# Attention scores: each head on 64 rows of TensorE, three products of high and low parts, a pair's heads in the two halves of the array's rows

## The chip, the cores and the metric

The kernel runs on one core of a Trainium2 chip. Five engines work side by side, each through its own list of instructions in order: TensorE (PE, with its weight loads shown apart as PEld), VectorE (DVE), ScalarE (ACT), GpSimd (POOL) and SyncE (SP), which here issues the DMAs. They wait for one another by semaphores. The metric is the time of one execution on the device in microseconds: before the change the median of three runs is 624.03 us (623.66 to 625.28).

## What is computed

Attention over 2 batches, 8 heads, 576 positions and 64 features a head, with a bias made by a small network from the distance of two positions; then two layers of the form w_out(gate(w_in x)) on the 1152 rows that come out, with 512 features and 2048 hidden ones.

```python
scores = q @ k.T / sqrt(64)                    # per batch and head, 576 x 576
psi_rel = log1p(abs(i - j)); psi_i = log1p(max(i, 1))
bias = relu((psi_rel / psi_i)[..., None] @ w1 + b1) @ w2      # 32 hidden, one value a head
attn = softmax(scores + bias)                  # minus the row's maximum, + 1e-9 below
x = (attn @ v) as 1152 rows of 512
h = x @ moe_w_in;  x = (h * sigmoid(1.702 * h)) @ moe_w_out
h = x @ moe2_w_in; x = (P(h) / Q(|h|)) @ moe2_w_out           # P cubic, Q quadratic
```

All is float32. Products in the two layers and in the scores are made from parts: a value is split into a high part, rounded to the type float32r that PE takes at full rate, and the low rest, and high x high, high x low and low x high are added up.

## The kernel before

**Stages.** First the bias table is made: 36 "beats" (`beat`), each with hidden values on DVE, POOL and ACT, four products on PE in column quarters of the array, an evacuation, and a DMA into a table in DRAM, from which bias tiles `bt` come back. Between and after the beats run 40 attention steps (loop over `s` in `attention_moe_moe`). Then the two layers follow. The conversion of their weights (`conv`, `split`) runs beside them, and five conversions fall into attention steps.

**A step.** The steps take pairs of heads (`hp`, 0 to 3), batches (`b`) and blocks of 128 queries in the order 4, 0, 1, 2, 3 (`QORDER`). Block 4 holds the last 64 queries of both heads in one unit; the others have two units, one a head. From step 15 on five steps in a row have one pair and batch. In this text a cycle is such a row: A (block 4, steps 15, 20, 25, 30, 35), B (16, 21, 26, 31, 36), C, D and E.

In its list for step s PE has, in this order: the transpose of the tail columns of step s - 3 (L288), the scores of step s (L223), products with values of earlier steps (L350 at full width, L347 in two column halves of the array, as many as have come due), and the transposes of the probabilities of step s - 3 (L315). The order in time is thus L288, L223, L350/L347, L315, L288 of the next step. Values come due in groups of five at the end of blocks 1 and 3; a B step has none.

**Score tiles.** A unit's scores lie in a `wide` tile, two PSUM banks with 288 columns each. There are two such tiles in turn; the one for the first unit of a step also takes the tail transpose. DVE reads a tile in L243 (scores plus bias, and the row's minimum of the negated sum), then ACT takes the exponential (L247). A tile may be written again when DVE has read it. A DVE step runs, in order: L230 (of the step before, needs ACT's second exponential), L243 for head 0, the reciprocal L257, copies of the tail transposes (L297, or two small ones in L301 where step s - 3 was block 4), L243 for head 1, low parts of attention's output (L373), a conversion if one is due, the low part of a key (L201) if one is due.

**The operands before.** The input `qk` has each head's queries twice, one copy in partitions 0 to 63 and one in 64 to 127, and the keys twice in the same way. `q_high` rounds the whole of the queries to `qT`; `q_low` then puts the low part into the lower 64 partitions. So a column of `qT` is the high part above the low part of the same query, and one product of it with the high keys `khi` (both copies) gives high x high + low x high; one with the low keys `klo` gives high x low + low x low. A unit takes 2 halves x 2 products on all 128 rows. In block 4 both heads come into one tile by columns that are zero for the other head: 2 x 4 products. Parts are made one or two such rows of steps ahead: POOL the queries (L182, L187), ACT the high keys (L193), DVE the low keys (L201).

Of the kernel before, what the change touches and what calls it, by code (L numbers as in the profile page):

```python
# [40 lines left out]
BR = BW + 15  # L41


QW = 1216


class Attention:
# [114 lines left out]
    def load_qk(self, pb, part=None):  # L162
        if pb < 8:
            if part in (None, 0):
                self.raw[pb] = self.op.tile([128, QW + 2 * S], F32, tag="qk", name="qk", bufs=2)
            n = (QW + 2 * S) // 4
# [7 lines left out]

    def new_parts(self, pb):
        p, bufs = (self.pp, 1) if pb == 1 else (self.op, 2)
        self.qT[pb] = p.tile([128, QW], F32R, tag="qT", name="qT", bufs=bufs)
        self.khi[pb] = p.tile([128, 2, S], F32R, tag="khi", name="khi", bufs=bufs)
        self.klo[pb] = p.tile([128, 2, S], F32R, tag="klo", name="klo", bufs=bufs)

    def q_high(self, pb):
        self.nc.gpsimd.tensor_scalar(out=self.qT[pb][:], in0=self.raw[pb][:, 0:QW], scalar1=1.0, scalar2=1.0,  # L182
                                     op0=ALU.mult, op1=ALU.mult)
# [5 lines left out]
    def k_raw(self, pb, a):  # L189
        return self.raw[pb][:, QW + S * a:QW + S * a + S]  # L190

    def k_high(self, pb, a):
        self.nc.scalar.activation(out=self.khi[pb][:, a, :], in_=self.k_raw(pb, a), func=AF.Copy, scale=-0.125)  # L193

    def k_low(self, pb, a):
        k, hi, lo = self.k_raw(pb, a), self.khi[pb][:, a, :].bitcast(F32), self.klo[pb][:, a, :]
        if 2 * pb + a in ():
            self.nc.gpsimd.tensor_scalar(out=k, in0=k, scalar1=-0.125, scalar2=1.0, op0=ALU.mult, op1=ALU.mult)
            self.nc.gpsimd.tensor_tensor(out=lo, in0=k, in1=hi, op=ALU.subtract)
        else:  # L200
            self.nc.vector.scalar_tensor_tensor(out=lo, in0=k, scalar=-0.125, in1=hi, op0=ALU.mult, op1=ALU.subtract)  # L201


    def scores(self, s):
        nc = self.nc
        hp, b, qc = self.steps[s]
        pb = 2 * hp + b
        q, khi, klo = self.qT[pb], self.khi[pb], self.klo[pb]

        if qc < 4:  # L210
            units = [[(128 * qc, 0)], [(704 + 128 * qc, 1)]]
        else:
            units = [[(512, 0), (576, 1)]]
# [12 lines left out]
    def sums(self, s):  # L226
        if 0 <= s < len(self.steps):
# [301 lines left out]
def attention_moe_moe(tc, t):  # L529
    nc = tc.nc  # L530
    new = tc.alloc_tile_pool
    A, M = Attention(tc, t), Moe(tc, t)
# [23 lines left out]
    A.bt, A.raw, A.v, A.qT, A.khi, A.klo = {}, {}, {}, {}, {}, {}  # L556
# [20 lines left out]
    def beat():  # L577
        i = beats[0]
        beats[0] += 1
        if i >= 41:  # L580
            return
        if i == 2:
            A.bias_setup2()
        if 3 <= i < 39:
            A.bias_out(A.rows[i - 3])
        if 2 <= i < 38:
            A.bias_matmul(A.rows[i - 2])
        if i < 36:
# [6 lines left out]
        if i in (4, 6, 8, 11, 13, 15):  # L595
            pb, j = divmod((4, 6, 8, 11, 13, 15).index(i), 3)
            A.q_low(pb, QW * j // 3, QW * (j + 1) // 3)
# [24 lines left out]
    for s in range(n + TLAG + 2):  # L622
# [35 lines left out]
        for piece in (('ea', 'to', 'qh', 'eb', 'ql', 'kh', 'xa', 'su', 'cv', 'pv', 'tr', 'xb', 'no', 'vo', 'kl', 'vl') if s < 12 else ('ea', 'vo', 'su', 'pv', 'eb', 'qh', 'ql', 'kh', 'xa', 'tr', 'no', 'to', 'xb', 'vl', 'cv', 'kl')):  # L658
# [15 lines left out]
                        A.q_high(x)  # L674
            elif piece == 'kh':
                for x, part in prep:
                    if part in (1, 2):
                        A.k_high(x, (1, 2).index(part))
            elif piece == 'kl':
                for x, part in prep:  # L680
                    if part in (1, 2):
                        A.k_low(x, (1, 2).index(part))
            elif piece == 'ql':
                for x, part in prep:
                    if part in (1, 3):
                        j = (1, 3).index(part)
                        c = (0, 608, 1216)
                        A.q_low(x, c[j], c[j + 1])
            elif piece == 'xa':
                A.exps(s, 0)  # L690
            elif piece == 'xb':
# [141 lines left out]
def _layout(v):  # L833
    import numpy as np

    f = np.float32
    qk = np.zeros((8, 128, QW + 2 * S), f)
    vv = np.zeros((8, 128, 640), f)
    for hp in range(4):
        for b in range(2):  # L840
            q, k, x = (np.asarray(v[n])[b, 2 * hp:2 * hp + 2] for n in "qkv")
            o, q, k = qk[2 * hp + b], q.transpose(0, 2, 1), k.transpose(0, 2, 1)
            for h in (0, 64):
                o[h:h + 64, 0:576] = q[0]
                o[h:h + 64, 640:704] = q[1, :, 512:]
                o[h:h + 64, 704:QW] = q[1, :, :512]
                o[h:h + 64, QW:QW + S] = k[0]
                o[h:h + 64, QW + S:] = k[1]
# [46 lines left out]
```

## Time and profile before

| | |
|---|---|
| runs | 624.03 us median (623.66 to 625.28) |
| profiled execution | 624.78 us, span of its instructions 623.0 us |
| PE, PEld busy | 94%, 79% of the span |
| DVE, ACT, POOL busy | 70%, 71%, 63% |
| score products (L223) | 320, 92.4 us busy summed over their two groups |
| low keys on DVE (L201), high keys on ACT (L193) | 16 of 0.808 us, 16 of 0.694 us |
| queries on POOL (L182, L187 of 64x608) | 8 of 1.274 us, 12 of 1.490 us |
| load of a pair's queries and keys | 1184.0 KB |
| granted clock of PE | 0.99 on average |

Busy time is the union of an engine's instructions. Matmuls are pipelined, so one lasts longer than the distance to the next: that distance, start to start, is what a product costs PE. A name like `wide<-khi,qT` says tile written, tiles read. "[0.76 <-PE wide L223]" behind an instruction means that its engine stood idle for 0.76 us before it and that the score product released it.

### The profile page before, as it was taken

How to read it: one execution, taken by the hardware profiler on the slowest of the kernel's cores; microseconds unless marked ns; L12 is line 12 of the kernel's file. 1: busy time of each engine (PE TensorE's matmuls, PEld its weight loads, DVE VectorE, ACT ScalarE, POOL GpSimd, SP SyncE). 2: the span in 40 equal slices, each digit the busy share in tenths (PEclk: the TensorE clock that was granted, in tenths of full speed). 3: DMA queues.
4: the chain of work that ended last, by engine and by line, in shares of the span. 5: the costliest groups of instructions: out<-in, count | busy, mean ns of one | idle time of the engine just before them, and what ended most of it. 6: DMA issues, size and time to landing. Idle time of an engine off the chain costs nothing.

```text
span 623.0 us, 10326 instructions
## 1 busy us (share of the span) xinstructions
PE 588.4 (94%) x3450; PEld 494.7 (79%) x3450; DVE 437.4 (70%) x913; ACT 443.2 (71%) x921; POOL 394.4 (63%) x452
## 2 busy tenths in 40 slices
PE   6986999999999898899999989998999999999997
PEld 2233477777777887899999988987988899989995
DVE  7999876888876888821112888868778666666663
ACT  6777787899987666642222666678888987878784
POOL 5867668799974667732223577756767765655663
PEclk9999899999999999999999999998999999999999
DMA  6689781936414567610001476630100100001001
GB/s 241 176 279 290 212 328 31 391 128 240 141 34 136 176 211 217 205 38 0 2 1 34 129 209 204 204 102 1 35 1 1 51 2 1 0 1 52 1 1 51
DMA packets 23909, 70.93 MB, mean 114 GB/s; under 512 B 2480, under 2 KB 2864, under 8 KB 22960
## 3 DMA queue, kind: packets, MB, share of 16 engines
q1 hardware_dynamic: 23712, 70.15, 34.5%
q8 instruction: 27, 0.44, 0.3%
q14 instruction: 26, 0.21, 0.1%
q10 hardware_dynamic: 144, 0.13, 0.1%
HBM read 57.01 MB, written 13.25 MB: 113 GB/s over the span
## 4 chain that ended last, share of the span: by engine, by line
PE 37%; DVE 14%; ACT 13%; issue 2%; POOL 0%; DVEq 0%; ACTq 0%
PE hps L446 18%; PE acc L525 12%; PE acc L518 6%; DVE tmp L418 5%; ACT up L422 3%; ACT w L434 3%; DVE sg L465 2%; DVE tmp L425 2%; DVE top L423 2%; ACT sg L464 2%; ACT ra L489 1%; ACT sq L481 1%; ACT ra L488 1%; ACT ra L487 1%; ACT ra L484 1%
## 5 line engine op out<-in xcount | busy, mean ns | idle before, releaser
L446 PE MATMUL hps<-xhi,w 128*128 128x384 f32 x768 | 153.5, 341 | 14.5 <-DVE sg L465 9.9
L446 PEld LDWEIGHTS hps<-xhi,w 128*128 128x128 f32 x768 | 136.1, 189 | 24.8 <-DVE sg L465 15.6
L435 POOL TENSOR_TENSOR w<-tmp,w 128x512 fp32r<-128x512 f32 x64 | 82.5, 1288 | 40.2 <-ACT w L434 34.1
L458 POOL TENSOR_TENSOR glo<-sg,ghi 128x384 fp32r<-128x384 f32 x48 | 48.9, 1018 | 64.3 <-PE acc L518 45.0
L446 PE MATMUL hps<-xlo,w 128*128 128x384 f32 x384 | 82.2, 335 | 0.0
L518 PE MATMUL acc<-ghi,w 128*128 128x384 f32 x384 | 76.7, 334 | 0.0
L525 PE MATMUL acc<-w,ghi 128*128 128x512 f32 x288 | 75.7, 393 | 0.0
L465 DVE TENSOR_TENSOR sg<-hps,sg 128x384 f32<-128x384 f32 x48 | 26.8, 558 | 65.5 <-ACT sg L464 65.5
L260 POOL TENSOR_SCALAR p<-p,mn 128x512 f32<-128x512 f32 x72 | 57.4, 808 | 22.4 <-DVE PTt L297 9.2
L498 POOL TENSOR_SCALAR ra<-ra,small 128x384 f32<-128x384 f32 x48 | 28.2, 587 | 66.5 <-ACT ra L487 66.5
L247 ACT ACTIVATE p<-p,mn 128x576 f32<-128x576 f32 x72 | 55.9, 778 | 18.8 <-DVE mn L243 10.9
L446 PEld LDWEIGHTS hps<-xlo,w 128*128 128x128 f32 x384 | 68.3, 189 | 0.0
L518 PEld LDWEIGHTS acc<-ghi,w 128*128 128x128 f32 x384 | 67.5, 188 | 0.0
L422 ACT ACTIVATE up<-raw 128x512 int32<-128x512 uint32 x59 | 37.8, 641 | 36.5 <-DVE tmp L418 33.7
L243 DVE CUSTOM_DVE_ANT_0 p<-wide,bt 128x576 f32<-128x576 f32 x72 | 54.1, 751 | 8.8 <-PE wide L223 6.9
L525 PEld LDWEIGHTS acc<-w,ghi 128*128 128x128 f32 x288 | 53.4, 188 | 8.6
L497 DVE TENSOR_TENSOR ra<-ra,hps 128x384 f32<-128x384 f32 x48 | 26.6, 555 | 37.4 <-ACT ra L489 37.3
L455 ACT CAST ghi<-sg 128x384 fp32r<-128x384 f32 x48 | 24.7, 514 | 38.2 <-DVE sg L465 19.8
L500 POOL TENSOR_TENSOR ra<-ra 128x384 f32<-128x384 f32 x48 | 48.7, 1015 | 4.1
L458 POOL TENSOR_TENSOR glo<-ra,ghi 128x384 fp32r<-128x384 f32 x48 | 48.8, 1017 | 2.5 <-PE acc L525 2.0
L223 PE MATMUL wide<-khi,qT 128*128 128x288 f32 x160 | 48.1, 323 | 1.4 <-ACT st L137 0.8
L464 ACT ACTIVATE sg<-hps 128x384 f32<-128x384 f32 x48 | 23.4, 487 | 30.7 <-PE hps L446 30.7
(95 smaller groups left out, 1285.0 us busy)
## 6 DMA issues: line engine op xcount, KB each, us to landing
raw<-win SPq DMA_DIRECT2D x32, 512.0 KB, 3.6
raw<-wout SPq DMA_DIRECT2D x32, 512.0 KB, 3.7
bias_all<-st SPq DMA_DIRECT2D x36, 295.5 KB, 3.7
bt<-bias_all SPq DMA_DIRECT2D x16, 576.0 KB, 6.0
qk<-qk SPq DMA_DIRECT2D x7, 1184.0 KB, 7.5
v<-v SPq DMA_DIRECT2D x8, 320.0 KB, 5.7
out<-o SPq DMA_DIRECT2D x8, 256.0 KB, 2.2
qk<-qk SPq DMA_DIRECT2D x4, 296.0 KB, 4.2
```

The lines of the kernel that those rows point to most:

```text
L223: nc.tensor.matmul(ps[:, half, 0:288], w, x, start=(i == 0), stop=(i == len(ops) - 1))
L243: nc.vector.tensor_tensor_reduce(out=pv.rearrange("p (x j) -> p x j", x=2), in0=ps[:, :, 0:288], in1=self.bt[qc][:, a, :].rearrange("p (x ...
L247: nc.scalar.activation(out=pv, in_=pv, func=AF.Exp, bias=mn[:, a:a + 1], scale=-1.0, accum_out=mn[:, 2 + a:3 + a])
L260: nc.gpsimd.tensor_scalar(out=p[:, a, 0:512], in0=p[:, a, 0:512], scalar1=r, scalar2=1.0, op0=ALU.mult, op1=ALU.mult)
L422: nc.scalar.activation(out=self.up[j].bitcast(I32), in_=lo, func=AF.Copy, scale=2.0 ** -29)
L435: nc.gpsimd.tensor_tensor(out=w[:, 2 * o + 1, :], in0=val, in1=w[:, 2 * o, :].bitcast(F32), op=ALU.subtract)
L446: nc.tensor.matmul(ps[:, 0:CH], w[:, wi, 128 * d:128 * d + 128], xx[:, d, :], start=(i == 0 and d == 0), stop=(i == 2 and d == 3))
L458: nc.gpsimd.tensor_tensor(out=glo[:], in0=g, in1=ghi[:].bitcast(F32), op=ALU.subtract)
L465: nc.vector.tensor_tensor(out=sg[:], in0=h, in1=sg[:], op=ALU.mult)
L500: nc.gpsimd.tensor_tensor(out=t0[0][:], in0=t0[0][:], in1=t0[1][:], op=ALU.add)
L518: nc.tensor.matmul(acc[e][:, 0:CH], w[:, wi, 128 * e:128 * e + 128], g[gi][:], start=(k == 0 and i == 0), stop=(k == NF - 1 and i == 2))
L525: nc.tensor.matmul(acc[e][:], g[gi][:, 128 * e:128 * e + 128], w[:, wi, :], start=(k == 0 and i == 0), stop=(k == NF - 1 and i == 2))
```

## The change

The input has each head once: head 0 of a pair in partitions 0 to 63, head 1 in 64 to 127, queries (640 columns, the last 128 with zeros where the column is the other head's) and keys (576). Tiles `q` and `k` hold the high and the low part side by side. A head's scores are three products a half (high x high, low x high, high x low) on its 64 rows, at row position 0 or 64 of the array; the two heads' products are issued in turn, each into its own tile. Block 4 takes all 128 rows and one tile, as before, with three products a half. Low x low is left out. High and low parts are made in fewer and partly wider operations, and the conversions within the beats and steps move to fewer places.

```diff
-QW = 1216
+QW = 640
     def load_qk(self, pb, part=None):
...
-                self.raw[pb] = self.op.tile([128, QW + 2 * S], F32, tag="qk", name="qk", bufs=2)
+                self.raw[pb] = self.op.tile([128, QW + S], F32, tag="qk", name="qk", bufs=2)
     def new_parts(self, pb):
         p, bufs = (self.pp, 1) if pb == 1 else (self.op, 2)
-        self.qT[pb] = p.tile([128, QW], F32R, tag="qT", name="qT", bufs=bufs)
-        self.khi[pb] = p.tile([128, 2, S], F32R, tag="khi", name="khi", bufs=bufs)
-        self.klo[pb] = p.tile([128, 2, S], F32R, tag="klo", name="klo", bufs=bufs)
+        self.q[pb] = p.tile([128, 2, QW], F32R, tag="q", name="q", bufs=bufs)
+        self.k[pb] = p.tile([128, 2, S], F32R, tag="k", name="k", bufs=bufs)
     def q_low(self, pb, a, b):
-        q = self.qT[pb][64:128, a:b]
-        self.nc.gpsimd.tensor_tensor(out=q, in0=self.raw[pb][64:128, a:b], in1=q.bitcast(F32), op=ALU.subtract)
+        q = self.q[pb][:, :, a:b]
+        self.nc.gpsimd.tensor_tensor(out=q[:, 1, :], in0=self.raw[pb][:, a:b], in1=q[:, 0, :].bitcast(F32),
+                                     op=ALU.subtract)
+    def k_high(self, pb):
+        self.nc.scalar.activation(out=self.k[pb][:, 0, :], in_=self.raw[pb][:, QW:], func=AF.Copy, scale=-0.125)
+    def k_low(self, pb):
+        k = self.k[pb]
+        self.nc.vector.scalar_tensor_tensor(out=k[:, 1, :], in0=self.raw[pb][:, QW:], scalar=-0.125,
+                                            in1=k[:, 0, :].bitcast(F32), op0=ALU.mult, op1=ALU.subtract)
     def scores(self, s):
...
-        for unit in units:
+        heads = [slice(0, 64), slice(64, 128)] if qc < 4 else [slice(0, 128)]
+        for _ in heads:
             ps, self.stile = self.stile, None
-            if ps is None:
-                ps = self.wide()
-            for half in range(2):
-                sl = slice(288 * half, 288 * half + 288)
-                ops = [(q[:, o:o + 128], k[:, a, sl]) for o, a in unit for k in (khi, klo)]
-                for i, (w, x) in enumerate(ops):
-                    nc.tensor.matmul(ps[:, half, 0:288], w, x, start=(i == 0), stop=(i == len(ops) - 1))
-            self.sp.append(ps)
+            self.sp.append(self.wide() if ps is None else ps)
+        for half in range(2):
+            for i, (x, y) in enumerate(((0, 0), (1, 0), (0, 1))):
+                for ps, p in zip(self.sp, heads):
+                    nc.tensor.matmul(ps[:, half, 0:288], q[p, x, 128 * qc:128 * qc + 128],
+                                     k[p, y, 288 * half:288 * half + 288], start=(i == 0), stop=(i == 2),
+                                     tile_position=(p.start, 0))
 def attention_moe_moe(tc, t):
...
-        if i in (6, 8, 13, 15):
-            A.k_low(i // 10, int(i in (8, 15)))
-        if i in (5, 7, 12, 14):
-            A.k_high(i // 10, int(i in (7, 14)))
+        if i in (6, 13):
+            A.k_high(i // 10)
+        if i in (7, 14):
+            A.k_low(i // 10)
...
             elif piece == 'kl':
                 for x, part in prep:
-                    if part in (1, 2):
-                        A.k_low(x, (1, 2).index(part))
+                    if part == 2:
+                        A.k_low(x)
```

On PE, at step 32 (a C step), these are the instructions in order before the change; a number behind a tile's name tells one buffer's use from another's, and "waits" names the engines whose semaphores an instruction waits for.

```order
L288 MATMUL wide_2029<-cst_99,ptl_1915 128x128 [waits DVE_49,PE_49,Pool_49]
L223 MATMUL wide_2029<-khi_1718,qT_1717 128x288
L223 MATMUL wide_2029<-klo_1719,qT_1717 128x288
L223 MATMUL wide_2029<-khi_1718,qT_1717 128x288
L223 MATMUL wide_2029<-klo_1719,qT_1717 128x288
L223 MATMUL wide_2035<-khi_1718,qT_1717 128x288 [waits DVE_49]
L223 MATMUL wide_2035<-klo_1719,qT_1717 128x288
```

The same place on PE with the change (L279 is the tail transpose, L213 the score product):

```order
L279 MATMUL wide_2090<-cst_99,ptl_1976 128x128 [waits DVE_49,PE_49,Pool_49]
L213 MATMUL wide_2090<-k_1766,q_1765 128x288
L213 MATMUL wide_2092<-k_1766,q_1765 128x288 [waits DVE_49]
L213 MATMUL wide_2090<-k_1766,q_1765 128x288
L213 MATMUL wide_2092<-k_1766,q_1765 128x288
L213 MATMUL wide_2090<-k_1766,q_1765 128x288
```

Before, four products go to the first tile and the fifth, first into the second tile, waits for DVE. Now the tiles alternate, and the wait for the second tile stands at the second of twelve products.

On DVE in the bias stage, where it makes hidden values (L98) and low parts of the keys (L201 before, L194 now):

```order
 L98 TENSOR_SCALAR room<-bc,nbm 128x560 x3
 L98 TENSOR_SCALAR room<-bc,nbm 128x544 x3
-L201 SCALAR_TENSOR_TENSOR klo<-qk,khi 128x576
 L98 TENSOR_SCALAR room<-bc,nbm 128x528 x2
-L607 MEMSET small 128x1
+L194 SCALAR_TENSOR_TENSOR k<-qk,k 128x576
+L597 MEMSET small 128x1
 L98 TENSOR_SCALAR room<-up,nbm 128x512 x2
-L201 SCALAR_TENSOR_TENSOR klo<-qk,khi 128x576
 L98 TENSOR_SCALAR room<-up,nbm 128x496 x2
```

One operation of the same size stands where two did; the same happens for each later pair.

## Rows read from the trace of the kernel before

**Rows 1.** The page's first part: busy time, share of the span, instructions.
```profile
PE 588.4 (94%) x3450; PEld 494.7 (79%) x3450; DVE 437.4 (70%) x913; ACT 443.2 (71%) x921; POOL 394.4 (63%) x452
```

**Rows 2.** Stages: stretch, its length, busy us (instructions) by engine, PE's clock, DMA.
```profile
20.00:40.00 20.00, 18.40 (x117) 5.76 (x116) 20.00 (x38) 14.93 (x27) 15.14 (x21) 1.00 0.74 212
...
90.70:122.04 31.34, 31.34 (x229) 23.08 (x228) 23.00 (x76) 25.32 (x60) 23.75 (x31) 1.00 0.56 213
153.97:169.89 15.92, 15.92 (x119) 12.17 (x118) 13.27 (x44) 14.81 (x37) 15.46 (x19) 1.00 0.46 165
```

**Rows 3.** Waits with PE waiting, 85 to 184 us: us in total, times, longest.
```profile
PE wide L288 <- DVE mn L230: 0.5, 1, 0.5
```

**Rows 4.** Order of time on PE, steps 31 to 34: start us, us, instruction.
```profile
157.19 0.38 PE L223 MATMUL wide<-khi,qT 128*128 128x288 f32 x1
157.41 0.29 PE L223 MATMUL wide<-klo,qT 128*128 128x288 f32 x1
...
158.20 0.29 PE L223 MATMUL wide<-klo,qT 128*128 128x288 f32 x1
...
159.33 0.38 PE L223 MATMUL wide<-khi,qT 128*128 128x288 f32 x1
...
159.94 0.32 PE L223 MATMUL wide<-khi,qT 128*128 128x288 f32 x1
...
160.35 0.29 PE L223 MATMUL wide<-klo,qT 128*128 128x288 f32 x1
...
163.30 0.38 PE L223 MATMUL wide<-khi,qT 128*128 128x288 f32 x1
...
164.30 0.29 PE L223 MATMUL wide<-klo,qT 128*128 128x288 f32 x1
...
166.27 0.38 PE L223 MATMUL wide<-khi,qT 128*128 128x288 f32 x1
...
167.29 0.30 PE L223 MATMUL wide<-klo,qT 128*128 128x288 f32 x1
```

**Rows 5.** Order of time on DVE: reads of the score tiles, steps 31 and 33.
```profile
158.09 0.76 DVE L243 CUSTOM_DVE_ANT_0 p<-wide,bt 128x576 f32<-128x576 f32 x1 [0.76 <-PE wide L223]
...
159.04 0.75 DVE L243 CUSTOM_DVE_ANT_0 p<-wide,bt 128x576 f32<-128x576 f32 x1
...
164.20 0.76 DVE L243 CUSTOM_DVE_ANT_0 p<-wide,bt 128x576 f32<-128x576 f32 x1
...
164.96 0.44 DVE L301 COPY PTt<-wide 64x64 f32<-64x64 f32 x2
165.43 0.76 DVE L243 CUSTOM_DVE_ANT_0 p<-wide,bt 128x576 f32<-128x576 f32 x1
```

**Rows 6.** Order of time on PE around value products in column halves, step 23.
```profile
132.45 0.29 PE L223 MATMUL wide<-klo,qT 128*128 128x288 f32 x1
132.67 0.49 PE L347 MATMUL xt<-PT,v 128*64 128x320 f32 x2
...
133.53 0.44 PE L347 MATMUL xt<-PT,v 128*64 128x320 f32 x2
133.90 0.33 PE L315 MATMUL pt<-cst,p 128*128 128x128 f32 x1
```

**Rows 7.** Order of time around step 2: a release and two waits for it.
```profile
41.20 0.08 DVE L243 DVE_READ_ACCUMULATOR2_ANT mn<- 128x1 f32 x1
...
41.58 0.29 PE L223 MATMUL wide<-klo,qT 128*128 128x288 f32 x1
...
42.93 0.40 PE L223 MATMUL wide<-khi,qT 128*128 128x288 f32 x1 [0.79 <-ACT st L137]
...
42.98 0.76 DVE L243 CUSTOM_DVE_ANT_0 p<-wide,bt 128x576 f32<-128x576 f32 x1
```

**Rows 8.** Groups by line and shape: busy us, mean ns of one, idle before.
```profile
L223 PEld LDWEIGHTS wide<-khi,qT 128*128 128x128 f32 x160 | 31.1, 194 | 3.8 <-ACT room L91 1.2 <-DVE mn L243 1.2 <-ACT st L137 1.0
...
L201 DVE SCALAR_TENSOR_TENSOR klo<-qk,khi 128x576 fp32r<-128x576 f32 x16 | 12.9, 808 | 0.0
```

More of the change, by code (lines that the diff above doesn't have):

```diff
@@ L164, in load_qk @@
             if part in (None, 0):
-                self.raw[pb] = self.op.tile([128, QW + 2 * S], F32, tag="qk", name="qk", bufs=2)
-            n = (QW + 2 * S) // 4
+                self.raw[pb] = self.op.tile([128, QW + S], F32, tag="qk", name="qk", bufs=2)
+            n = (QW + S) // 4
             sl = slice(0, 4 * n) if part is None else slice(n * part, n * part + n)
@@ L176, in new_parts @@
         p, bufs = (self.pp, 1) if pb == 1 else (self.op, 2)
-        self.qT[pb] = p.tile([128, QW], F32R, tag="qT", name="qT", bufs=bufs)
-        self.khi[pb] = p.tile([128, 2, S], F32R, tag="khi", name="khi", bufs=bufs)
-        self.klo[pb] = p.tile([128, 2, S], F32R, tag="klo", name="klo", bufs=bufs)
+        self.q[pb] = p.tile([128, 2, QW], F32R, tag="q", name="q", bufs=bufs)
+        self.k[pb] = p.tile([128, 2, S], F32R, tag="k", name="k", bufs=bufs)
     def q_high(self, pb):
-        self.nc.gpsimd.tensor_scalar(out=self.qT[pb][:], in0=self.raw[pb][:, 0:QW], scalar1=1.0, scalar2=1.0,
+        self.nc.gpsimd.tensor_scalar(out=self.q[pb][:, 0, :], in0=self.raw[pb][:, 0:QW], scalar1=1.0, scalar2=1.0,
                                      op0=ALU.mult, op1=ALU.mult)
     def q_low(self, pb, a, b):
-        q = self.qT[pb][64:128, a:b]
-        self.nc.gpsimd.tensor_tensor(out=q, in0=self.raw[pb][64:128, a:b], in1=q.bitcast(F32), op=ALU.subtract)
[L189 to L201, printed above, removed]
+        q = self.q[pb][:, :, a:b]
[7 more added lines that the diff above has]
+                                            in1=k[:, 0, :].bitcast(F32), op0=ALU.mult, op1=ALU.subtract)
     def scores(self, s):
@@ L207, in scores @@
         pb = 2 * hp + b
[L208 to L213, printed above, removed]
+        q, k = self.q[pb], self.k[pb]
+        heads = [slice(0, 64), slice(64, 128)] if qc < 4 else [slice(0, 128)]
         self.sp = []
-        for unit in units:
+        for _ in heads:
             ps, self.stile = self.stile, None
-            if ps is None:
-                ps = self.wide()
-            for half in range(2):
-                sl = slice(288 * half, 288 * half + 288)
-                ops = [(q[:, o:o + 128], k[:, a, sl]) for o, a in unit for k in (khi, klo)]
-                for i, (w, x) in enumerate(ops):
-                    nc.tensor.matmul(ps[:, half, 0:288], w, x, start=(i == 0), stop=(i == len(ops) - 1))
-            self.sp.append(ps)
+            self.sp.append(self.wide() if ps is None else ps)
[5 more added lines that the diff above has]
+                                     tile_position=(p.start, 0))
     def sums(self, s):
@@ L555, in attention_moe_moe @@
     A.bd = dp.tile([S * H * BR + 16], F32, name="bias_all")
-    A.bt, A.raw, A.v, A.qT, A.khi, A.klo = {}, {}, {}, {}, {}, {}
+    A.bt, A.raw, A.v, A.q, A.k = {}, {}, {}, {}, {}
     A.P, A.mn, A.PT = {}, {}, {}
@@ L594, in beat @@
             A.q_high(i // 10)
-        if i in (4, 6, 8, 11, 13, 15):
-            pb, j = divmod((4, 6, 8, 11, 13, 15).index(i), 3)
-            A.q_low(pb, QW * j // 3, QW * (j + 1) // 3)
-        if i in (6, 8, 13, 15):
-            A.k_low(i // 10, int(i in (8, 15)))
-        if i in (5, 7, 12, 14):
-            A.k_high(i // 10, int(i in (7, 14)))
+        if i in (5, 8, 12, 15):
+            A.q_low(i // 10, 0 if i in (8, 15) else 320, 320 if i in (8, 15) else 640)
+        if i in (6, 13):
+            A.k_high(i // 10)
+        if i in (7, 14):
+            A.k_low(i // 10)
         if i in (21, 26, 34):
@@ L676, in attention_moe_moe @@
                 for x, part in prep:
-                    if part in (1, 2):
-                        A.k_high(x, (1, 2).index(part))
+                    if part == 1:
+                        A.k_high(x)
             elif piece == 'kl':
                 for x, part in prep:
-                    if part in (1, 2):
-                        A.k_low(x, (1, 2).index(part))
+                    if part == 2:
+                        A.k_low(x)
             elif piece == 'ql':
@@ L685, in attention_moe_moe @@
                     if part in (1, 3):
-                        j = (1, 3).index(part)
-                        c = (0, 608, 1216)
-                        A.q_low(x, c[j], c[j + 1])
+                        A.q_low(x, 320 if part == 1 else 0, 640 if part == 1 else 320)
             elif piece == 'xa':
@@ L836, in _layout @@
     f = np.float32
-    qk = np.zeros((8, 128, QW + 2 * S), f)
+    qk = np.zeros((8, 128, QW + S), f)
     vv = np.zeros((8, 128, 640), f)
@@ L842, in _layout @@
             o, q, k = qk[2 * hp + b], q.transpose(0, 2, 1), k.transpose(0, 2, 1)
[L843 to L848, printed above, removed]
+            for a in range(2):
+                h = slice(64 * a, 64 * a + 64)
+                o[h, 0:512] = q[a, :, :512]
+                o[h, 512 + 64 * a:576 + 64 * a] = q[a, :, 512:]
+                o[h, QW:] = k[a]
             vv[2 * hp + b, :, :512] = x[:, :512].reshape(2, 4, 128, D).transpose(2, 1, 0, 3).reshape(128, 512)
```

## The prediction, made before the changed kernel was run

> **What bounds the kernel now.** The page's busy line gives PE 94% of the span, the others 63 to 71% [rows 1], but a busy PE says little by itself, so I cut the span into the kernel's own stages. Three matter. In 20 to 40 us, where the bias table is made, DVE is busy for all of the 20 us and PE is not. From 90.70 us (step 11) to 169.89 us (step 35) PE is busy without a gap, ACT and POOL for over 90% of the later rows [rows 2]. The list of waits with PE as the waiting engine has, from 85 to 184 us, one entry of 0.5 us in all [rows 3]: there each step ends when PE is through its list, and what PE gains or loses is gained or lost by the kernel. After attention the two gated layers run in their own order and only begin sooner or later; the change touches nothing there.
>
> Then one cycle of five steps in PE's order of time [rows 4], 15.92 us long: A (one unit of two heads, query block 4), B, C, D, E (two heads each). In a step's eight score products the starts stand 0.132 us apart (157.41 to 158.20, six intervals). B is the short step: it starts at 157.19, has no value products, and C starts 2.14 later. Against it stand DVE's two reads of the score tiles [rows 5]: head 0's begins at 158.09, while head 1's products still run; head 1's begins 0.95 later and ends at 159.79. C's fifth product, the first that writes the tile head 1 lay in, starts at 159.94: only 0.15 later. So PE is the bound, but at the short step DVE is hardly behind it. That interleaving, head 0 finished halfway, is what the change gives up.
>
> **The change, part by part.** *Products.* A unit with one head had 2 x 2 products on 128 rows; now a head has 2 x 3 on 64 rows, and the two heads are issued in turn. If two such run together, a step takes six slots instead of eight: 2 x 0.132 = 0.264 us saved per step, also in A, where six products on all rows replace eight. For steps 11 to 39 that is 29 x 0.264 = 7.7 us. Do two halves run together? The trace has no row halves, but column halves: two value products start together at 132.67 and two more at 133.53, and the last two take 0.44 together, hardly more than one [rows 6]. I take row halves to behave likewise.
>
> *Changes of array shape.* Before, scores, transposes and the tail transpose shared one shape, and only the value products had another. Where shapes change, the next product starts 0.22 after the last score product (132.45 to 132.67) instead of 0.13, and the first pair lasts 0.49 where a later one lasts 0.44. Back again it is 133.53 to 133.90, 0.37, against 0.29 between pairs ((133.53 - 132.67)/3) [rows 6]. So a change costs about 0.09 + 0.05; call it w = 0.15, with 0.05 (only the longer first product) and 0.25 (the 0.16 by which a product's 0.29 outlasts its slot, and 0.09) as ends. The new scores add a change at the entry of each two-headed step, and one at the exit where transposes or the full-width value product follow, since an exit to column halves was a change already. Per cycle that is 4 + 3.
>
> *The wait that moves.* Before, the first four products write one tile and the fifth waits for the other tile to be read. Now the second of twelve waits for it. Queued behind it on PE are ten products, then values and transposes; ACT's copies of the transposes and DVE's next first read wait for those. Also DVE's first read now waits for the whole step. I walk one cycle, times from B's start, first for B. First pair effectively at 0.09 + w (before, 0.09: 157.41 less 0.132), last pair 0.66 later at 0.90, end 1.19 (0.29 each), first read 1.31 (0.12 after the end, as 158.09 stands to the fourth product, which started at 157.68 and took 0.29). The second read ends 1.70 after the first begins [rows 5]: 3.01. Now C: a product behind such a wait is effectively under way 0.17 after the release (41.28, end of the read's accumulator, to 41.58 less 0.132 [rows 7]). So 3.18, and C's last pair starts at 3.84, where C's last product started at 160.35 - 157.19 = 3.16: 0.68 late. The exit adds w: D starts 0.83 late. D needs no wait, and its last pair is at 0.90 for 1.00, so E is 0.72 late by PE; but D's second read ends 1.99 after its first begins (164.20 to 166.19, two small copies lie between), at 1.31 + 1.99 = 3.30 from D's start, and E's last pair then starts at 3.30 + 0.17 + 0.66 = 4.13 where it started at 167.29 - 163.30 = 3.99. E is 0.97 late, its exit makes 1.12, A gives back 0.26: **0.86 us lost per cycle**. In general 0.26 + 4w; even changes of shape for nothing would not make it a gain.
>
> Four cycles (20 to 39) lose 3.4. Steps 11 to 19 (31.34 us, [rows 2]) have longer steps between and one short step, 13. The same walk gives -0.78 + 8w = +0.4. Together 0.26 + 24w: 3.9 us, and 1.5 to 6.3 for the ends of w.
>
> *The bias stage.* DVE makes the low part of the keys in 8 instead of 16 operations of 0.81 us [rows 8]. Three of those that go lie before step 11, at most 2.4 us of a full DVE. Against it: at step 2 head 1's tile comes free only for the product at 42.93, and head 0's read follows at 42.98 [rows 7]; it would now begin 0.11 + 0.66 + 0.29 + 0.12 after 42.93, at 44.11, 1.1 later. In the steps that follow each other directly (7, 8) the second read and the next first read are now at least 0.17 + 0.66 + 0.29 + 0.12 = 1.24 apart; I put 0.4 on each, an estimate. I take -2.4 + 1.1 + 0.8 = -0.5, with -2.4 and +2 as ends.
>
> *Taken at nothing:* the halved load of queries and keys on SP's queue, ACT's high parts of the keys (8 fewer), POOL's high and low parts of the queries (fewer elements; the low part in a shape the trace lacks, 128x320 for 64x608). All end before PE asks for them [rows 3]; without that cover they would be gains.
>
> Sum: 3.9 - 0.5 = +3.4 on the profiled execution's 624.78 us (span 623.0 and 1.8 around it), 628.2. The median of the runs is 0.75 lower, so **627.4**.
>
> **Rivals.** *(1) PE alone decides: faster.* If reads end before PE asks, a short step costs no wait, and only products less changes count: 7.7 - 39w (23 entries and 16 exits). With w between the row's 0.15 and its low end, 0.10, that is -3.8, with the bias part -4.3: 619.7. For it: one PE wait in 99 us, and outside the short step and the one after it the second tile is free well before it is asked for. Against it: the 0.15 us margin at C. It decides as soon as DVE's second read ends about 0.7 us sooner than in my walk, for instance because PE's lead moves to another step.
>
> *(2) The halves don't run together,* so the change doesn't do what it says. Twelve slots of 0.132: a step's last product at 1.69, B's second read ends at 3.67, C is 2.0 late; the same walk gives 3.5 per cycle, 14 for four, 5 for steps 11 to 19, and 1 in the bias stage: +20, 644. For it: no row shows row halves. Against it: the column halves.
>
> *(3) A head's next weights load only after its product.* Today products on the same rows follow at 0.132 although each has a load of 0.19 [rows 4, 8], so loads hide beneath products of the same rows. If that fails for halves, a pair takes 0.132 and some 0.11 (of the 0.17 behind a release): six of 0.24, last pair at 1.44, 3.0 per cycle, 12 for four, 4.5 and 1: +17, 641. For it: halves load in turn, twelve loads where there were eight. Against it: those rows. The Trainium skill ("TensorE: Matmul & The Clock Gate", Part 3, What overlaps and what doesn't) says that a weight load overlaps running products only where their row groups differ; that would be this rival. By that rule the trace should not show 0.132 today, so I give it little.
>
> **How the numbers follow.** Forecast 0.62 at 627.4, its own range 624.5 to 630; rival 1 0.25 at 619.7; rival 2 0.07; rival 3 0.06. The range of 617.5 to 632 leaves out rivals 2 and 3 and the outermost of rival 1, some 0.16 to 0.19. The bound of what can be told is 0.3%, 1.9 us: below 622.2 or above 625.9. Most of rival 1 is faster, and a little of the forecast (a dear gain in the bias stage): 0.27. Of the forecast about a quarter lies within, with w near 0.05 to 0.10, and the slow end of rival 1: 0.18. The rest, 0.55, is slower.
>
> **What would show it.** Right: two score products with starts a few ns apart, one on each tile; PE waits named after DVE's second read, about 0.8 us at the step after B and 0.3 at E; cycles near 16.8 us instead of 15.92; first reads 0.4 us later in their step. Rival 1: cycles below 15.9 and no such wait. Rival 2: starts of all twelve 0.13 apart. Rival 3: pairs 0.24 apart with loads between. Wrong altogether: the stage before step 11 or the two layers after attention change by more than 2 us, or PE's granted clock falls in steps 11 to 39, where it is 1.00 now [rows 2].

## The result

The changed kernel takes 629.4 us, median of four runs (629.05 to 630.97), against 624.54 of the kernel before (four runs): a ratio of 1.0083, 95% interval 1.0060 to 1.0106, so 5 us slower. The forecast was 627.4, and 629.4 lies near the slow end of its own range. The profiled execution took 630.97 (span 629.2), 6.2 more than the one of before. Where these 6.2 us arise is read from the start of each step's score products, after less before, in the two traces:

| step | 2 | 3 | 10 | 20 | 25 | 30 | 35 | 39 | span |
|---|---|---|---|---|---|---|---|---|---|
| after - before, us | -3.30 | -1.74 | -1.27 | -0.21 | +1.60 | +3.50 | +5.39 | +6.12 | +6.2 |

Up to step 10 (the bias stage) 1.3 us are gained, steps 10 to 39 lose 7.4, and the two layers change nothing.

The page's first part, the three stages of [rows 2] (20 to 40 us, steps 11 to 19, one cycle from step 30 to 35), and the waits of PE:

```profile
PE 591.3 (94%) x3562; PEld 488.2 (78%) x3562; DVE 430.6 (68%) x905; ACT 439.6 (70%) x913; POOL 375.0 (60%) x450
```
```profile
20.00:40.00 20.00, 16.31 (x105) 5.24 (x105) 19.53 (x40) 16.05 (x32) 12.81 (x23) 1.00 0.82 246
89.73:121.86 32.13, 31.93 (x254) 21.36 (x253) 20.87 (x74) 24.13 (x57) 19.39 (x31) 1.00 0.48 171
157.50:175.31 17.81, 16.98 (x132) 11.37 (x133) 13.65 (x43) 14.35 (x36) 12.57 (x19) 1.00 0.39 144
```
```profile
PE wide L279 <- DVE PTt L288: 2.9, 6, 0.7
PE pt L306 <- ACT PT L322: 0.4, 2, 0.2
```

POOL has 19 us less to do than before [rows 1], and its share of a cycle falls from 15.46 of 15.92 us [rows 2] to 12.57 of 17.81. PE, which before was busy through the whole cycle, now idles 0.83 us of it at full clock, and its listed waits behind DVE are 2.9 us in place of 0.5 [rows 3], all at the tail transpose; a wait inside a step's row of score products does not stand in this list. A cycle is 17.8 us; forecast was 16.8.

PE's order of time over that cycle, for [rows 4]:

```profile
160.41 0.27 PE L279 MATMUL wide<-cst,ptl 128*128 128x128 f32 x1
160.61 1.05 PE L213 MATMUL wide<-k,q 64*128 64x288 f32 x12
...
163.19 1.41 PE L213 MATMUL wide<-k,q 64*128 64x288 f32 x12
...
167.63 1.06 PE L213 MATMUL wide<-k,q 64*128 64x288 f32 x12
...
170.54 1.38 PE L213 MATMUL wide<-k,q 64*128 64x288 f32 x12
...
173.49 1.09 PE L306 MATMUL pt<-cst,p 128*128 128x128 f32 x8
175.25 0.30 PE L279 MATMUL wide<-cst,ptl 128*128 128x128 f32 x1 [0.67 <-DVE PTt L288]
```

Twelve products take 1.05 us, six pairs: 5 x 0.13, 0.1 for the longer first one, and 0.29 for the last. The halves run together. Where PE must wait for the second tile (C at 163.19, E at 170.54) they take 1.41 and 1.38: 0.35 of waiting each. And A, the step after E, does not start its tail transpose until 175.25, 0.67 after the transposes of E are done. DVE's two reads before C's products, for [rows 5]:

```profile
161.79 0.76 DVE L234 CUSTOM_DVE_ANT_0 p<-wide,bt 128x576 f32<-128x576 f32 x1 [0.47 <-PE wide L213]
...
162.74 0.74 DVE L234 CUSTOM_DVE_ANT_0 p<-wide,bt 128x576 f32<-128x576 f32 x1
```

The first starts only when the whole step's products are through (161.67), the second ends at 163.49 with its accumulator, and C's second product starts at 163.55, 0.36 after its first: the wait that the prediction put there. For the wait behind E the rows of DVE and POOL, first before (step 34 starts at 166.27), then after (it starts at 170.54):

```profile
168.08 0.15 DVE L230 TENSOR_SCALAR mn<-mn 128x2 f32<-128x2 f32 x1
```
```profile
164.57 1.48 POOL L187 TENSOR_TENSOR qT<-qk,qT 64x608 fp32r<-64x608 f32 x1
166.15 2.56 POOL L260 TENSOR_SCALAR p<-p,mn 128x512 f32<-128x512 f32 x2
...
169.04 1.28 POOL L435 TENSOR_TENSOR w<-tmp,w 128x512 fp32r<-128x512 f32 x1
```
```profile
172.93 1.24 DVE L221 TENSOR_SCALAR mn<-mn 128x2 f32<-128x2 f32 x1
174.09 0.74 DVE L234 CUSTOM_DVE_ANT_0 p<-wide,bt 128x576 f32<-128x576 f32 x1
```
```profile
167.94 0.87 POOL L186 TENSOR_TENSOR q<-qk,q 128x320 fp32r<-128x320 f32 x1
169.85 1.36 POOL L251 TENSOR_SCALAR p<-p,mn 128x512 f32<-128x512 f32 x2 [1.04 <-DVE mn L248]
...
172.85 1.31 POOL L426 TENSOR_TENSOR w<-tmp,w 128x512 fp32r<-128x512 f32 x1 [0.84 <-ACT w L425]
```

Before, POOL was behind: low part, normalising, and only then (169.04) the subtraction that splits a converted weight; DVE's addition of 1e-9 to two columns of numbers had been done at 168.08 in 0.15 us. After, POOL's low part is 0.6 us shorter, it stands ready when the normalising can begin and again when the weight's high part is there, and starts the subtraction at 172.85, 0.08 us ahead of DVE's addition. That now lasts 1.24 us, and it ends 0.02 us after the subtraction (174.15 and 174.18). Step E's first read of a score tile starts 1.1 us late, and the chain of reads, tail copy and tail transpose carries it to PE. A weight is converted in steps 23, 28 and 33, and the addition lasts 1.24 us each time; the steps E behind them (24, 29, 34) are 4.77, 4.80 and 4.77 us long where they were 3.63, 3.63 and 3.65.

The trace of before has the same hold in another place, behind POOL's low part of the queries, in step 4 (and, 1.15 us long, in step 11), so its price could be read there:

```profile
59.58 1.47 POOL L187 TENSOR_TENSOR qT<-qk,qT 64x608 fp32r<-64x608 f32 x1
```
```profile
59.61 1.47 DVE L230 TENSOR_SCALAR mn<-mn 128x2 f32<-128x2 f32 x1
```

### The profile page after: what moved, and what is told of

Same layout as the page of the kernel before. It is cut to its first block, busy times and chain, and to the rows that moved or that the text cites. A ratio compares the mean times of both kernels' runs of the same rounds, so it can differ in the third digit from the quotient of the medians.

```text
span 629.2 us, 10515 instructions
## 1 busy us (share of the span) xinstructions
PE 591.3 (94%) x3562; PEld 488.2 (78%) x3562; DVE 430.6 (68%) x905; ACT 439.6 (70%) x913; POOL 375.0 (60%) x450
## 4 chain that ended last, share of the span: by engine, by line
PE 36%; DVE 14%; ACT 13%; issue 2%; POOL 0%; DVEq 0%; ACTq 0%
PE hps L437 18%; PE acc L516 12%; PE acc L509 6%; DVE tmp L409 5%; ACT up L413 3%; ACT w L425 3%; DVE sg L456 2%; DVE tmp L416 2%; DVE top L414 2%; ACT sg L455 2%; ACT ra L480 1%; ACT sq L472 1%; ACT ra L479 1%; ACT ra L478 1%; ACT ra L475 1%
## 5 line engine op out<-in xcount | busy, mean ns | idle before, releaser
L251 POOL TENSOR_SCALAR p<-p,mn 128x512 f32<-128x512 f32 x72 | 51.8, 730 | 46.1 <-DVE PTt L288 23.0
L213 PE MATMUL wide<-k,q 64*128 64x288 f32 (+1 forms) x432 | 48.9, 319 | 2.1 <-ACT st L137 1.2
L213 PEld LDWEIGHTS wide<-k,q 64*128 64x128 f32 (+1 forms) x432 | 36.9, 191 | 11.4 <-DVE mn L234 3.4
```

The lines of the kernel that those rows point to most:

```text
L213: nc.tensor.matmul(ps[:, half, 0:288], q[p, x, 128 * qc:128 * qc + 128], k[p, y, 288 * half:288 * half + 288], start=(i == 0), stop=(i == ...
L251: nc.gpsimd.tensor_scalar(out=p[:, a, 0:512], in0=p[:, a, 0:512], scalar1=r, scalar2=1.0, op0=ALU.mult, op1=ALU.mult)
```

## The experiments

The theory has two parts. **Collision:** about a third of the loss is POOL's subtraction holding DVE's small addition. **Waits:** the rest is PE waiting for the second tile at the short step and after it, and changes of array shape. The table gives each kernel's median, its ratio to the kernel before (which ran beside each, 624.15 to 624.62), what steps 10 to 39 cost in its profile against before, and the lengths of steps 24, 29 and 34.

| kernel | median us | ratio, 95% interval | steps 10 to 39 | E steps |
|---|---|---|---|---|
| changed | 629.40 | 1.0083 (1.0060 to 1.0106) | +7.4 | 4.77, 4.80, 4.77 |
| conversions in C | 627.67 | 1.0056 (1.0042 to 1.0070) | +5.1 | 4.07, 3.92, 3.91 |
| values even | 633.23 | 1.0149 (1.0133 to 1.0165) | +8.1 | 4.77, 4.78, 4.77 |
| heads in turn | 631.72 | 1.0128 (1.0107 to 1.0150) | +9.4 | 4.40, 4.41, 4.38 |
| both of the first two | 636.33 | 1.0192 (1.0179 to 1.0205) | +11.6 | 5.17, 3.91, 5.17 |
| low part three times | 627.86 | 1.0051 (1.0032 to 1.0070) | +5.1 | 4.08, 4.08, 3.90 |
| no small addition | 627.25 | 1.0038 (1.0023 to 1.0053) | +4.6 | 3.90, 3.90, 3.90 |
| that, values even | 627.75 | 1.0045 (1.0029 to 1.0060) | +3.3 | 3.77, 3.77, 3.76 |
| before, low part left out | 627.11 | 1.0037 (1.0020 to 1.0053) | +2.4 | 4.41, 4.43, 4.42 |
| no addition, tails first | 626.70 | 1.0043 (1.0029 to 1.0058) | +3.9 | 3.81, 3.82, 3.82 |
| that, values even | 625.54 | 1.0017 (1.0008 to 1.0027) | +2.9 | 3.73, 3.75, 3.74 |
| before, the same three | 626.15 | 1.0038 (1.0021 to 1.0056) | +2.0 | 3.68, 3.68, 3.68 |

The intervals of "conversions in C" and "low part three times" overlap with that of the changed kernel, so these two are told from it by the last two columns and not by the medians alone.

### Conversions one step earlier

```
-  for _ in range(n - s in (3, 7, 12, 17, 21) ...     # weight conversions
+  for _ in range(n - s in (3, 8, 13, 18, 21) ...
-  if part == 2:                        # low part of the keys
+  if part == (3 if s >= 20 else 2):
```

> Changed kernel, with the three weight conversions of steps 23, 28 and 33 (D) made one step earlier (C), and the low key parts made one step later to make room on DVE. Theory (collision: DVE's 1.24 us on 128x2 numbers lies inside POOL's two-input subtraction of the weight split, so step E's first read and with it PE comes about 1.1 us late, in three cycles): about 3 us faster than the changed kernel, 626, and no PE wait of 0.6 us behind the tail copy at step E. Rival (the conversion's own DVE work is what makes the step late, wherever it stands): it only moves to the step after, 0 to 1 us faster, 628.4 to 629.4.

Measured: 627.67, 1.7 us less, and in the profile 2.2 us less over steps 10 to 39. The addition at E is short again:

```profile
169.10 0.15 DVE L221 TENSOR_SCALAR mn<-mn 128x2 f32<-128x2 f32 x1
```

E is 3.9 to 4.1 us long and two of the three cycles are 16.95 and 16.97, close to the 16.8 of the prediction. The gain is smaller than the 3 us expected, since E without a collision is 0.87 shorter and not 1.1: PE's own work takes over first.

### Value products spread evenly, and with the first edit

```
-  for _ in range(5 if s >= n or len(pv) > 5 else ... 3 if pv and pv[0][1] == 4 else 2):
+  for _ in range(5 if s >= n or len(pv) > (6 if s >= 15 else 5) else 3 if s < 15 and pv and pv[0][1] == 4 else 2):
```

> Changed kernel, with the value products from step 15 on spread two chunks a step over all five steps, so that the short step B is no longer without them; the same instructions in all. Theory (the second of twelve products waits at C and E for the second tile since B is too short for DVE's two reads): the wait at C goes, 0.5 to 0.9 us a cycle, over four cycles 2 to 4 us faster than the changed kernel, 625.5 to 627.5. Rival (the loss is the changes of array shape, which this does not touch, or even one more of them in B): no change or up to 1 us slower, 629 to 630.5.

> Both edits together: conversions one step earlier and value products spread two a step. Theory (two separate losses, collision and short step): the gains add, 5 to 7 us faster than the changed kernel, 622.5 to 624.5, at or just below the kernel before. Rival (both edits ease one and the same wait): no more than the larger of the two alone, 625.5 to 627.

Both were wrong: 633.23 and 636.33, slower than the changed kernel. The wait at C did go (its products take 1.06 again), but B with value products is 3.14 us in place of 2.60 and C only 0.88 shorter, so the two steps gain 0.3. In both kernels 2.6 to 2.8 us are lost behind step 39, where more value products are left over and the first layer starts later. And the collision came at more places: also in step 38 of both, and in the second in each D behind a conversion:

```profile
168.40 1.24 DVE L221 TENSOR_SCALAR mn<-mn 128x2 f32<-128x2 f32 x1
```
```profile
168.02 1.59 POOL L426 TENSOR_TENSOR w<-tmp,w 128x512 fp32r<-128x512 f32 x1 [0.55 <-ACT w L425]
```

Here POOL began 0.4 us ahead (its subtraction itself took 1.59 in place of 1.28), and those steps D are 4.5 us long in place of 2.91, with a wait of 1.4 us on PE. In steps 24 and 34 the granted clock stands at its lower level (0.50, 1.2 GHz) for 3.4 us soon after that wait, and E is 5.17 us long; in step 29, at 1.00, it is 3.91. So in this kernel some 2.5 us of the 11.6 are clock, an estimate (2 x 1.26). Moving the conversion only shifts when the two meet; a few tenths decide.

### Heads one after the other

```
-  for half in range(2):
-      for i, (x, y) in enumerate(((0, 0), (1, 0), (0, 1))):
-          for ps, p in zip(self.sp, heads):
+  for ps, p in zip(self.sp, heads):
+      for half in range(2):
+          for i, (x, y) in enumerate(((0, 0), (1, 0), (0, 1))):
```

> Changed kernel, with head 0's six products issued first and then head 1's six, so that no two halves stand side by side; the same products. Theory (a pair of halves side by side takes one slot of 0.132 us): twelve slots in place of six, 0.53 us more than the eight of before in each of 23 two-headed steps from step 10 on, 0.26 less in six others, and the changes of shape 39 x 0.15: 16.5 us over before from step 10 on, where the changed kernel has 7.4; 638. Rival (side by side brings little, since the step is set by DVE's two reads): 629 to 631, or less, since head 1's tile is asked for later.

Measured: 631.72, between the two. The theory's 638 was wrong about the array:

```profile
163.30 1.43 PE L213 MATMUL wide<-k,q 64*128 64x288 f32 x12
```

Twelve in a row would take 11 x 0.132 + 0.29 = 1.74; here it is 1.43, against 1.05 in pairs. By the spacing of the single records and the two signals at the ends of the heads, head 0's six start at 163.30, .54, .67, .79, .93 and 164.07, and head 1's at 163.67, .91, 164.05, .18, .31 and .44: head 1's first product, issued seventh, started ahead of head 0's fourth. The records do not name the head; which is which is read from two regular rows of starts 0.13 apart and from the weight load that waits for the second tile, at 163.67. So 0.37 us a step are lost where PE is the bound (D is 3.28 for 2.91) and nothing where it waits anyway: C is 4.46 for 4.43, because the later second tile costs its 0.35 of waiting no more, and E is 4.40 for 4.77. From step 20 to 35 this kernel takes 53.51 us, the changed one 53.45; it is slower in steps 10 to 19 (1.5 us) and before.

### The collision, approached from four sides

More work for POOL in D, without the small addition, and before with less work for POOL:

```
   elif piece == 'ql': ...  if part in (1, 3):
+      for _ in range(3 if part == 3 else 1):
           A.q_low(...)
```
```
-  A.sums(s - 1)
-  nc.vector.reciprocal(out=mn[:, 6:6 + nu], in_=mn[:, 4:4 + nu])
+  nc.vector.reciprocal(out=mn[:, 6:6 + nu], in_=mn[:, 2:2 + nu])
```
```
   # kernel before
-  if part in (1, 3):
+  if part == 1 or (part == 3 and s < 20):
       ... A.q_low(...)
```

> Changed kernel, with POOL's low part of the queries in step D written three times over in place of once: 1.7 us more work for POOL in each cycle, the same results. Theory (POOL, relieved, comes to the weight split just as DVE comes to its small addition, and holds it 1.24 us): with POOL later, the addition goes first, step E is 3.9 us long in place of 4.8 in three cycles, and more work makes the kernel 2.2 to 2.7 us faster than the changed one, 626.7 to 627.2. Rival (POOL's load as such delays what follows): 629.4 or slower, up to 632.

> Changed kernel without DVE's small addition (1e-9 to sums that are at least 1, which changes no sum in fp32); the reciprocal reads the sums themselves. Theory (POOL's two-input operation holds only the small operation on two operands in SBUF, not the read of the score tile out of PSUM): step E 3.9 us in place of 4.8, 2.5 to 3 us faster than the changed kernel, 626.4 to 626.9. Rival (POOL holds whatever DVE brings next): the first read at E starts as late as now, no change, 629 to 629.4.

> Kernel before, scores untouched, with POOL's low part of the queries in step D left out from step 20 on (the low parts of half the query columns are then missing from the output). Theory (the collision needs nothing of the new scores, only POOL early at the weight split): the small addition is held 1.2 us in steps 23, 28 and 33, E is longer by up to 1.1 us in three cycles, and with less work the kernel is 2 to 3 us slower, 626 to 627. Rival (the collision needs the later reads of the new scores as well): no change, 623.8 to 624.5.

Measured: 627.86, 627.25 and 627.11. Giving POOL 1.7 us more to do in a cycle makes the kernel 1.5 us faster by the medians and 2.3 over steps 10 to 39; taking 1.5 us from POOL in the kernel before, with its old scores, makes it 2.5 us slower. All three lie on the theory's side, 0.1 to 0.7 us above its ranges. The three profiles, first DVE and POOL with the low part three times, then DVE and POOL without the addition, then DVE and POOL of before with the low part left out:

```profile
169.92 0.15 DVE L221 TENSOR_SCALAR mn<-mn 128x2 f32<-128x2 f32 x1
```
```profile
165.26 2.76 POOL L186 TENSOR_TENSOR q<-qk,q 128x320 fp32r<-128x320 f32 x3
168.00 2.55 POOL L251 TENSOR_SCALAR p<-p,mn 128x512 f32<-128x512 f32 x2
...
170.89 1.28 POOL L426 TENSOR_TENSOR w<-tmp,w 128x512 fp32r<-128x512 f32 x1
```
```profile
169.82 0.69 DVE L416 SCALAR_TENSOR_TENSOR tmp<-raw,tmp 128x512 uint32<-128x512 uint32 x1
170.43 0.75 DVE L234 CUSTOM_DVE_ANT_0 p<-wide,bt 128x576 f32<-128x576 f32 x1
```
```profile
170.37 1.28 POOL L426 TENSOR_TENSOR w<-tmp,w 128x512 fp32r<-128x512 f32 x1 [0.87 <-ACT w L425]
```
```profile
169.12 1.24 DVE L230 TENSOR_SCALAR mn<-mn 128x2 f32<-128x2 f32 x1
170.28 0.74 DVE L243 CUSTOM_DVE_ANT_0 p<-wide,bt 128x576 f32<-128x576 f32 x1
```
```profile
169.06 1.28 POOL L435 TENSOR_TENSOR w<-tmp,w 128x512 fp32r<-128x512 f32 x1 [0.86 <-ACT w L434]
```

With POOL late, the order is that of before: addition at 169.92, subtraction at 170.89. Without the addition, the read of the score tile out of PSUM starts at 170.43, while POOL's subtraction runs (170.37 to 171.65), and takes its usual 0.75: POOL holds the small operation, not the read. And the old scores show the same 1.24 us as soon as POOL is early, at 0.06 us ahead. That is cause and effect from both sides. The size in the changed kernel is 2.3 to 2.8 us of the 7.4.

The Trainium skill ("SBUF — State Buffer", SBUF: two separate sides) states that VectorE and GpSimd share one pair of ports as an exclusive lock: of a GpSimd operation and a VectorE operation that is in a two-port mode or has two inputs in SBUF, whichever starts first keeps the pair for its whole length, and the other is blocked in full. This case agrees for the addition: 1.24 us for an operation of 0.15, ending 0.02 to 0.03 us after POOL's. In which mode the addition runs no trace here shows.

### What is left: waits or changes of shape

```
-  'xa', 'tr', 'no', 'to', 'xb'     # first read .. tail copy, second read
+  'to', 'xa', 'tr', 'no', 'xb'
```

The even spread of value products was tried on top of the kernel without the addition and on top of this one, and all three edits on the kernel before. In the last two of these the spread ends with step 34, so that nothing more is left over behind step 39.

> As the kernel without the small addition, and with the value products spread two chunks a step. Theory (in the run with even value products the gain at C was there, 0.3 us over B and C, and was lost to the collision, which then also stood in step 38): cycles of 16.2 to 16.5 us in place of 16.95, four of them, 624 to 625.5, level with the kernel before. Rival (the extra change of shape in B eats what the wait gives): cycles of 16.9, 626.5 to 627.

> Changed kernel without the small addition, and from step 12 on DVE copies the transposed tails (0.27 us, in step D two copies, 0.44) before the first read of a step instead of between the two reads; the same work. Theory (what is left of the loss is PE's waits for the tiles that DVE reads: in a cycle about 0.37 us at the tail transpose before C, 0.35 at C's second product, 0.33 at E's): tiles come free 0.2 to 0.45 us sooner, 0.4 to 0.7 us a cycle, cycles of 16.2 to 16.5 in place of 16.9, 624.5 to 625.7. Rival (the rest is changes of array shape): cycles stay at 16.9, 627 to 627.5.

> The same, and value products two a step from step 15 to 34. Theory (waits and collision gone, PE's own work decides; PE's cycle is 5 x 0.26 shorter by the pairs and 7 or 8 changes of shape of 0.17 longer): cycles of 15.9 to 16.2, 622.5 to 624.5, level with or just below the kernel before. Rival (an eighth change of shape in B and what is left of the waits): cycles of 16.4 or more, 625 to 626.

> Kernel before with the same three edits (no small addition, tails copied first, values two a step from 15 to 34), scores untouched. Theory (it waits for no tile in steps 11 to 39, so there is nothing to gain): within 1 us of the kernel before, 623.5 to 625.2, a change of shape more in B against a little in the bias stage. Rival (the edits are good in themselves): 1.5 us or more faster.

Measured: 627.75, 626.70, 625.54 and 626.15. In the first, cycles are 16.5 to 16.7 us, between theory and rival, and 2.6 us are lost again behind step 39; no gain in all. The second lies between its two, the third where its rival had it, and the fourth is slower than both of its own. With the tails first, cycles are 16.77 in place of 16.93: less than the theory's 0.4 to 0.7. The wait moved:

```profile
157.98 0.30 PE L279 MATMUL wide<-cst,ptl 128*128 128x128 f32 x1
158.21 1.47 PE L213 MATMUL wide<-k,q 64*128 64x288 f32 x12
```
```profile
156.87 0.29 DVE L288 COPY PTt<-wide 128x128 f32<-128x128 f32 x1 [2.08 <-PE wide L213]
157.08 0.75 DVE L234 CUSTOM_DVE_ANT_0 p<-wide,bt 128x576 f32<-128x576 f32 x1
```

The tail transpose waits no more, but the twelve products take 1.47, 0.42 of waiting. The copy was not free early: it waits for the score products too, at 156.87, and starts the first read 0.25 after the products' end where it was 0.12. The last two are the cleanest pair, three cycles each, from step 20 to 35:

```profile
118.89:168.46 49.57, 49.03 (x397) 33.31 (x395) 36.77 (x111) 42.06 (x102) 38.78 (x53) 1.00 0.43 146
```
```profile
120.22:169.71 49.49, 49.15 (x355) 36.31 (x353) 39.60 (x115) 44.04 (x106) 45.04 (x53) 1.00 0.51 179
```

PE is busy 99% of both, so here PE's own work is compared: 49.57 with the new scores, 49.49 with the old, 0.03 us a cycle apart (with 0.23 a cycle of waiting left at E in the new one). With these edits the kernel before itself has cycles of 16.5 for 15.92: its PE waits for next to nothing in either, and B is 1.06 us longer, C 0.55 shorter. So the even spread costs 0.55 us a cycle of PE's own time. More changes of shape are the likely reason, but no run shows this by itself; the expectations had it too small. Before with the edits is 1.9 us slower than before, where within 1 us was expected. No version beat the kernel before.

## Why the prediction was right, and which step of it failed

The direction and the main mechanism were right; one step, costed at nothing, was not nothing, and one term was too small.

- **Halves run together:** right. The two products of a pair start 3 to 4 ns apart, twelve take 1.05 us; rivals 2 and 3 (0.13 and 0.24 a slot) fall.
- **Changes of shape,** w = 0.15: measured 0.18 at an entry (A's length falls by 0.09 where six products in place of eight give 0.26; D's by 0.06 to 0.08) and 0.14 at the exit to transposes: the first transpose starts 0.217 after the last product in place of 0.131, and the next 0.165 after that in place of 0.109. The exit to the full-width value product costs 0.19 (0.216 and 0.374 in place of 0.132 and 0.269). Four entries and three exits make 1.2 us a cycle, nearly the whole gain of 5 x 0.264.
- **The wait that moves:** right in place, nearly in size. In the cycle above, against B's start: C's last pair 0.54 late (forecast 0.68), D's start 0.91 (0.83), E's start by PE 0.85 and its last pair 0.92 (0.97). Without the collision a cycle costs 1.0 us (16.93 to 16.95), forecast 0.86. Part of the wait (0.3 to 0.45 us) stands ahead of C's first product, which the walk left out: in the cycle above between B's transposes, behind ACT's copy of them, in the other three at the tail transpose, behind DVE's copy. With 0.35 at C and 0.33 at E that is 1.0 to 1.1 us of waiting, about what the cycle costs, since the shapes eat the saving. The sign given for it, waits of PE named after DVE's second read, did not show: the list names the tail copy. First reads came 0.28 us later in their step (B), forecast 0.4.
- **E to A: the failed step.** The walk had A 1.12 late; it was 1.97. The sentence was "Taken at nothing: ... POOL's high and low parts of the queries (fewer elements ...). All end before PE asks for them". That was true of the queries and beside the point: what POOL does *next* starts earlier, and it met DVE. 0.85 us in each of three cycles, the forecast's missing 2.3 to 2.8 us.
- **Steps 10 to 39:** forecast 3.9, measured 7.4; without the collision 4.6 to 5.1, of which three cycles 3 x 1.0, steps 35 to 39 0.7 and steps 10 to 19 0.9 to 1.0, where 0.4 was put.
- **The bias stage:** -0.5 forecast. The low parts of the keys are 8 operations of the same length as the 16 of before [rows 8]:

```profile
L194 DVE SCALAR_TENSOR_TENSOR k<-qk,k 128x576 fp32r<-128x576 f32 x8 | 6.5, 811 | 0.0
```

 By step 2 the gain is 3.3 us, 1.6 are given back at step 2 (forecast 1.1), and at step 10 it is 1.3 in this profile, and 2.6 to 3.3 in three of the variants whose code is the same up to there. The spread goes with PE's clock, if not in proportion: each execution has some microseconds at the lower level in this stage, not at the same place, 10 in this profile and 6.8, 6.8 and 3.4 in the three. Before, it stands between 60 and 70 us; in the changed kernel's profile over 40 to 70:

```profile
60.00:70.00 10.00, 9.56 (x55) 4.80 (x47) 9.10 (x20) 5.76 (x13) 6.82 (x10) 0.66 0.71 199
```
```profile
40.00:50.00 10.00, 7.46 (x64) 3.40 (x60) 8.81 (x22) 6.29 (x15) 5.89 (x12) 0.84 0.73 203
50.00:60.00 10.00, 7.00 (x57) 2.80 (x57) 8.17 (x23) 7.93 (x17) 6.12 (x11) 0.83 0.89 286
60.00:70.00 10.00, 9.65 (x68) 4.25 (x65) 8.94 (x19) 6.57 (x14) 7.09 (x12) 0.83 0.70 202
```

(The last column but two is the granted clock: 0.66 over 10 us is 6.8 us at 1.2 of 2.4 GHz, 0.84, 0.83 and 0.83 are 10.) The two variants with as much of the lower level as before, 6.8 us, gain 2.6 and 3.2. The medians differ by 4.9, which is 7.4 less about 2.5 of the bias stage, an estimate. So the term put at -0.5 was about 2 us too small, the two misses had opposite signs, and that the forecast was 2 us off rather than 3.5 is luck. By the prediction's own sign (a change of more than 2 us before step 11) the three variants speak against its account of this stage, the changed kernel's own profile does not.

- **Rival 1** (PE alone decides, 619.7): its condition did not hold, and by the last pair above the gain it promised was too large. With nearly all waits gone the new scores are level with the old; without the 0.23 still left at E they would be 0.2 us a cycle faster, an estimate, and that with five changes of shape a cycle, since the even spread puts column halves behind B and E.

## What to carry to other kernels

A cost "taken at nothing" because its engine has slack must be followed one step on: ask what that engine does next, when it now does it, and whether a small operation of another engine on the critical chain then falls into it. When a wait moves from the fifth to the second of a step's products, walk the cycle with the readers' times, as was done here; the walk held to 0.15 us up to E. Look in the trace you have for the same pair of engines meeting: here it stood in step 4. And count the changes of array shape before packing halves: seven of 0.14 to 0.2 us ate what six slots in place of eight gave in five steps.

## What the runs showed of the hardware

- DVE's addition on 128x2 numbers takes 0.15 us alone. In all 48 places of the traces where it lasts over 0.5 us, it ends 0.02 to 0.03 us after an operation of POOL that started before it: 1.24 us behind the weight's subtraction, 1.15 and 1.47 behind the low part of the queries in the kernel before. On 128x1 numbers (block 4) it takes 0.15 beside POOL's normalising too (at 125.10 in the changed kernel, POOL from 125.01 to 125.71). Where the one on 128x2 took 0.15 beside a normalising in the kernel before, as at 168.08, POOL's operation lasted 1.1 us in place of 0.69. DVE's read of a score tile, PSUM with one operand in SBUF, is not held: all 72 of each kernel last 0.73 to 0.76 us.
- Products on the two row halves are not kept in the order of issue: the seventh, on the other half, started ahead of the fourth. Strict alternation gives 1.05 us for twelve, one head after the other 1.43, not 1.74.
- A product on half the rows starts 0.20 us after a full-array transpose, where one on all rows starts after 0.03; its first pair lasts 0.40 in place of 0.38.
- Products on float32r parts, 288 columns each, start 0.132 us apart at a granted clock of 1.00 [rows 2, 4]: 0.9 of a column per cycle of 2.4 GHz. No run here has products of another type beside them.
